# Three score visits instead of four for each two groups, in an attention and gated feed-forward kernel

## The chip, the cores and the metric

The kernel runs on one core of one Trainium2 chip. The metric is the device time of one execution in microseconds (us), as the median of several runs. Times "from the block's start" below count from the first gate matmul of a token block.

## The reference

Attention with a sliding window of 128 and four sink tokens for 4 batches of 8 heads, 768 tokens, head size 64. Its output, turned to 3072 tokens of 512 features, goes through a gated feed-forward layer (512 to 1536 and back).

```python
scores = scale * np.matmul(q, k.transpose(0, 1, 3, 2))
keep = is_sink | ((rel >= 0) & (rel < window))        # rel = query - key, window 128
a = softmax(np.where(keep, scores, -1e9))
x = np.matmul(a, v)                                   # to (3072, 512)
g = x @ w_gate
out = (g * sigmoid(g) * (x @ w_val)) @ w_out          # (3072, 512)
```

## The kernel before, in words

**Groups and blocks.** Attention is done in twelve groups of 256 queries (three to a batch: group g is batch g // 3, part c = g % 3). The feed-forward layer is done in eight token blocks of 256 or 512 tokens. A block of 512 has twelve *gate units* (function `gate`) and four *downs* (function `down`). A gate unit projects one chunk of 128 features with the gate weights into a bank `pg` (four matmuls of 512 columns on TensorE, called PE), takes tanh of it on ScalarE (ACT) into `th`, projects with the value weights into `pv`, and on VectorE (DVE) forms `u` from `th` and `pg`, and `ht` from `u` and `pv`. A down sums twelve matmuls over `ht` into `pd`.

**Attention between units.** The work of later groups is put by hand into numbered slots of a block's units. A slot's steps are issued between the two projections of its unit, so in each engine's queue they stand after `pg` and before `pv`. The steps of a group are:

- *Scores*, `step_S` (matmuls at L288, exps at L295, masks at L300). Eight heads are four pairs. Head size 64 fills half of PE's rows, so the two heads of a pair run in the two row halves. Each head has its own PSUM bank `s`. ACT takes exp of each head into `e`; a DVE multiplication by the mask, one for each pair, is put into the list `later`. Groups with c = 0 have no previous keys and take 384 columns for each head where the others take 512.
- *Sink scores*, `step_K` (L316), for groups with c > 0: one bank `pk` and one exp into `es`.
- *Values*, `step_PV` (L351), in four parts (two query tiles j, two halves hh of the heads). For c > 0 the first part also issues the sinks' matmuls (`step_sinks`, L331, 32 rows), which take four banks `o` at once; for c = 0 each part takes its own. DVE then divides (`rcp` L359, `xn` L365), through `later`.
- *Turning* the result, `step_X`: for these groups a transposing DMA on SP's queue from `xn` to `xT`, also through `later`. `xbar` turns a later group's q and k on the same queue.

`gate` calls `flush` after its own DVE work, which issues what is in `later`: masks, divisions and turns stand behind `u` and `ht` of their unit.

**Banks.** All PSUM tiles (`pg`, `pv`, `pd`, `s`, `pk`, `o`) come from one pool of eight banks. A tile that finds none free waits, on PE, for one that is released by its last reader.

**Order around the change.** Blocks 3, 4 and 5 carry groups 5 and 6, 7 and 8, 9 and 10. The order is written by `pair`, into slots:

```python
((s, s + 2), Ss(ga)), (s, [K(ga)]), ((s + 4, s + 5, s + 6, s + 7), PVs(ga)),
((s + 6, s + 8), Ss(gb)), ((s + 8, s + 9), Xs(ga)), (s + 6, [K(gb)]),
(10, 10, 11, 12) PVs(gb), (12, 13) Xs(gb)            # s = 0 everywhere
```

So scores are at units 0, 2, 6 and 8, two pairs of heads at each; the first group's values at 4, 5, 6 and 7; the second's at 10, 11 and the first down. In block 3 the first two units are of half the tokens and twice the features; their costs are alike.

Of the kernel before, what the change touches and what calls it, by code (L numbers as in the profile page):

```python
# [7 lines left out]
FP32 = mybir.dt.float32  # L8
BF16 = mybir.dt.bfloat16
AF = mybir.ActivationFunctionType  # L10
ALU = mybir.AluOpType
# [3 lines left out]
def kernel(  # L15
# [12 lines left out]
    nc = tc.nc  # L28
    P = 128
    B, H, S, D = q.shape  # L30
# [8 lines left out]
    NP2 = H // 2  # L39
    GC = S // 256  # L40
# [10 lines left out]
    scale = 1.0 / float(D) ** 0.5  # L51

    def pool(name, bufs, psum=False):
        if psum:
            return ctx.enter_context(
                tc.tile_pool(name=name, bufs=bufs, space=bass.MemoryType.PSUM))
        return ctx.enter_context(tc.tile_pool(name=name, bufs=bufs))
# [7 lines left out]
    epool = pool("epool", 2)  # L65
# [12 lines left out]
    def bank(shape, dtype, name):  # L78
        return psum.tile(shape, dtype, tag="b", name=name)
# [65 lines left out]
    mask = const.tile([P, 2, 256], BF16)  # L145
    mask0 = const.tile([P, 2, 256], BF16)
# [56 lines left out]
    kTs, qTs, es_t, e_t, xns, xTs = {}, {}, {}, {}, {}, {}  # L203
    later = []

    def flush():
        for f in later:
            f()
        later.clear()
# [60 lines left out]
            op=ALU.mult)  # L270
        vsbs.append(vsb)

    def step_S(g, p2):
        b, c = divmod(g, GC)
        if p2 == 0:
            e_t[g] = epool.tile([P, H, 512], BF16, tag="e", name="e")
        q0 = c * 256
        parts = [(q0, q0, 256, P), (q0 + P, q0 + P, P, 3 * P)]
        if c > 0:
            parts.insert(0, (q0 - P, q0, P, 0))  # L280
        lo = 0 if c > 0 else P
        pss = [bank([P, 512], FP32, "s") for _ in range(4)]
        for pp in range(2):
            p = 2 * p2 + pp
            for kk, qq, n, col in parts:
                for h in range(2):
                    r = slice(h * D, (h + 1) * D)
                    nc.tensor.matmul(  # L288
                        pss[2 * pp + h][:, col:col + n], kTs[b][r, p, kk:kk + P],
                        qTs[b][r, p, qq:qq + n], start=True, stop=True)  # L290
        m = (mask if c > 0 else mask0).rearrange("q (o a) x -> q o (a x)", o=1)
        for pp in range(2):
            h0 = 4 * p2 + 2 * pp
            for h in range(2):
                nc.scalar.activation(  # L295
                    e_t[g][:, h0 + h, lo:512], pss[2 * pp + h][:, lo:512],
                    AF.Exp, scale=scale)

            def dve(e=e_t[g][:, h0:h0 + 2, lo:512]):
                nc.vector.tensor_tensor(  # L300
                    e, e, m[:, :, lo:512].broadcast_to([P, 2, 512 - lo]), op=ALU.mult)
            later.append(dve)

    def step_K(g):
        b, c = divmod(g, GC)
        if c == 0:
            return
        ps = bank([P, P], FP32, "pk")
        kfl = kss.rearrange("q b p x -> q b (p x)")
        for a in range(2):  # L310
            for j in range(2):
                for hh in range(2):
                    r, p = 32 * (2 * j + hh), 2 * hh + a
                    t0 = c * 256 + j * P
                    k0 = (KW + 2 * NS) * p - 2 * NS * a
                    nc.tensor.matmul(  # L316
                        ps[r:r + KW], kfl[:, b, k0:k0 + KW], qTs[b][:, p, t0:t0 + P],
                        start=(a == 0), stop=(a == 1), skip_group_check=True)
        es_t[g] = espool.tile([P, P], BF16, tag="es", name="es")
        nc.scalar.activation(es_t[g], ps, AF.Exp, scale=scale)  # L320
# [54 lines left out]
    def step_X(g, j, evict="v"):  # L375
        t0 = g * 256 + j * P
        tb = max(i for i in range(len(SIZES)) if OFF[i] <= t0)
        off = t0 - OFF[tb]
        if tb == 0 and off == 0:
            xTs["01"] = xtp.tile([P, DMC, 512], BF16, tag="xT", name="xT")  # L380
            xTs[0], xTs[1] = (xTs["01"][:, :, 256 * i:256 * (i + 1)] for i in range(2))
        elif tb > 1 and off == 0:
            xTs[tb] = dense(xtp.tile([P, DMC * 512], BF16, tag="xT", name="xT"),
                            DMC, SIZES[tb])
            if tb == 3:
                for i in range(2):
                    xTs[tb, i] = xTs[tb][:, :, 256 * i:256 * (i + 1)]
        if g not in PEX:
            def sp():
                nc.sync.dma_start_transpose(xTs[tb][:, :, off:off + P], xns[g, j])  # L390
            later.append(sp)
            return
        pt = bank([P, DMC, P], BF16, "px")
        for i in range(DMC):
            nc.tensor.transpose(pt[:, i], xns[g, j][:, i * P:(i + 1) * P], ident)

        if evict == "a":
            nc.scalar.copy(out=xTs[tb][:, :, off:off + P], in_=pt)
            return

        def dve():
            nc.vector.tensor_copy(out=xTs[tb][:, :, off:off + P], in_=pt)
        if evict == "now":
            dve()
        else:
            later.append(dve)
# [99 lines left out]
    def gates(tb):  # L506
        return [(gate, tb, f) for f in range(0, DFC, 512 // SIZES[tb])]

    def downs(tb):
        return [(down, tb, t) for t in range(SIZES[tb] // P)]  # L510

    def A(fn, *a):
        return lambda: fn(*a)
# [2 lines left out]
        return [A(step_TN, g, i, j, evict) for j in range(2) for i in range(2)]  # L516

    def Ss(g):
        return [A(step_S, g, p2) for p2 in range(2)]

    def PVs(g):
        return [A(step_PV, g, j, hh) for hh in range(2) for j in range(2)]

    def Xs(g):
        return [A(step_X, g, j) for j in range(2)]
# [11 lines left out]
    def K(g):  # L537
        return A(step_K, g)

    def weave(us, slots):  # L540
        assert all(i < len(us) for i in slots)
        for i, (fn, tb, x) in enumerate(us):
            fn(tb, x, slots.get(i, []))

    def slots(*pairs):
        sl = {}
        for at, steps in pairs:
            for i, step in zip(at if isinstance(at, tuple) else (at,) * len(steps),
                               steps):
                sl.setdefault(i, []).append(step)  # L550
        return sl
# [92 lines left out]
    step_PV(0, 0, 0)  # L644
    step_PV(0, 0, 1)
    flush()
    step_S(1, 0)
    masks1 = list(later)
    later.clear()
    step_PV(0, 1, 0)  # L650
# [2 lines left out]
    step_X(0, 0)  # L653
    flush()
    step_X(0, 1, "now")
    step_S(1, 1)
    step_K(1)
    later[:0] = masks1
    flush()
# [12 lines left out]
    def NV(g):  # L672
        return L(A(load_nat, g), A(load_v, g))

    weave(us, slots(
        (4, TN(2)[::2]), (5, TN(2)[1::2]), ((6, 7), Ss(2)), (6, [K(2)]),
        ((8, 8), PVs(2)[:2]), (9, [A(step_PV, 2, 0, 1, "a"), A(step_PV, 2, 1, 1, "a")]),
        ((10, 11), [A(step_X, 2, 0, "a"), A(step_X, 2, 1, "a")]),
        (11, [NV(4), lambda: nc.gpsimd.tensor_copy(out=vcl[64:128], in_=vcl[0:64])]),
        ((14, 14, 15, 15), TN(3, "aa")),  # L680
        (15, [A(xbar, 4)]), (15, [NV(5)]), (19, [A(xbar, 5)]),
        ((17, 18), Ss(3)), (18, [A(step_ks, 1)]), (18, [A(step_vsb, 1)]),
        ((19, 19, 19, 20), PVs(3)), (20, Xs(3)),
        (19, [L(Ss(4)[0], K(4))]), (20, Ss(4)[1:]),
        ((21, 21, 21, 22), PVs(4)), (21, Xs(4)[:1]),
        (22, [Xs(4)[1], flush, A(behind, 3, 383), A(load_nat, 6)]),
        (23, [A(xbar, 6), A(turned, 6), A(load_v, 6), NV(7)])))

    def pair(ga, gb, sh=0):
        s = sh  # L690
        return [((s, s + 2), Ss(ga)), (s, [K(ga)]),
                ((s + 4, s + 5, s + 6, s + 7), PVs(ga)),
                ((s + 6, s + 8), Ss(gb)), ((s + 8, s + 9), Xs(ga)), (s + 6, [K(gb)]),
                ((12, 12, 13, 13) if s else (10, 10, 11, 12), PVs(gb)),
                ((14, 14) if s else (12, 13), Xs(gb))]

    weave([(gate, (3, i), 0) for i in range(2)] + gates(3)[2:] + downs(3), slots(
        (15, [A(step_ks, 2), A(step_vsb, 2)]), *pair(5, 6), (9, [flush, A(xbar, 7)]),
        (13, [flush, A(behind, 4, 511), NV(8)]),
        (15, [A(xbar, 8)]), (15, [NV(9)])))  # L700
    weave(gates(4) + downs(4), slots(
        *pair(7, 8), (3, [A(xbar, 9)]), (15, [A(step_ks, 3), A(step_vsb, 3)]),
        (3, [NV(10)]), (15, [A(xbar, 10)]), (15, [NV(11)])))
    weave(gates(5) + downs(5), slots(*pair(9, 10), (6, [A(xbar, 11)])))
    us = gates(6) + gates(7) + downs(6) + downs(7)
    us[-1] = (lambda tb, t, a: down(tb, t, a, True), *us[-1][1:])
    weave(us, slots(
# [36 lines left out]
```

## Time and profile before

| | us |
|---|---|
| median of 4 runs | 238.38 (237.97 to 238.97) |
| the profiled execution | 239.01 |
| its span, first to last instruction | 237.2 |
| gate units of block 3, from 75.73 to 101.07 | 25.34 |
| gate units of block 4, from 111.67 to 138.11 | 26.44 |
| gate units of block 5, from 148.72 to 173.89 | 25.17 |
| downs after each of them | 10.60 |

The profile gives each engine's instructions in order of time. In a timeline line the columns are the start in us, the time covered, engine and source line, operation, output and input with shapes, the count of instructions merged, and in square brackets the idle time before it with what ended it. PEld is PE's loading of weights. The TensorE clock granted is 1.0 throughout. Matmuls overlap in the pipeline, so a start is surer than an end: costs of PE are read from start to start.

### The profile page before, as it was taken

How to read it: one execution, taken by the hardware profiler on the slowest of the kernel's cores; microseconds unless marked ns; L12 is line 12 of the kernel's file. 1: busy time of each engine (PE TensorE's matmuls, PEld its weight loads, DVE VectorE, ACT ScalarE, POOL GpSimd, SP SyncE). 2: the span in 40 equal slices, each digit the busy share in tenths (PEclk: the TensorE clock that was granted, in tenths of full speed). 3: DMA queues.
4: the chain of work that ended last, by engine and by line, in shares of the span. 5: the costliest groups of instructions: out<-in, count | busy, mean ns of one | idle time of the engine just before them, and what ended most of it. 6: DMA issues, size and time to landing. Idle time of an engine off the chain costs nothing.

```text
span 237.2 us, 4880 instructions
## 1 busy us (share of the span) xinstructions
PE 229.6 (97%) x1867; PEld 128.0 (54%) x1893; DVE 157.6 (66%) x333; ACT 113.6 (48%) x235; POOL 74.9 (32%) x100
## 2 busy tenths in 40 slices
PE   7999999999999999999999999999999999999994
PEld 4677645696555644444444544444444445488443
DVE  3897889677651898970798980688970598877000
ACT  3795475556552845512845622655622663333221
POOL 8985875722602307403526350080000000000000
PEclk9999999999999999999999999999999999999999
DMA  7999999994998968995999997599204100200132
GB/s 136 160 182 177 182 198 205 157 145 73 152 231 150 149 74 56 151 129 162 135 128 129 137 144 154 137 92 143 44 16 137 70 3 0 44 4 0 45 133 91
DMA packets 108743, 27.62 MB, mean 116 GB/s; under 512 B 95792, under 2 KB 105776, under 8 KB 108720
## 3 DMA queue, kind: packets, MB, share of 16 engines
q0 software_dynamic: 76640, 13.90, 76.9%
q1 hardware_dynamic: 30672, 11.58, 25.5%
q10 hardware_dynamic: 1408, 1.84, 2.5%
q8 instruction: 15, 0.25, 0.4%
q14 instruction: 8, 0.07, 0.1%
HBM read 28.34 MB, written 6.29 MB: 146 GB/s over the span
## 4 chain that ended last, share of the span: by engine, by line
PE 91%; DVE 2%; DMA 2%; ACT 1%; issue 1%; SPq 0%; DVEq 0%; ACTq 0%
PE pv L416 26%; PE pd L496 26%; PE pg L416 25%; PE o L351 4%; PE s L288 4%; DMA st<-in_k_dram 2%; DVE xn L365 1%; PE pt L572 1%; PE pt L226 1%; PE o L331 1%; PE pn L241 1%; PE pk L316 1%; ACT th L436 1%; PE s L589 1%; DVE rcp L359 0%
## 5 line engine op out<-in xcount | busy, mean ns | idle before, releaser
L444 DVE SCALAR_TENSOR_TENSOR u<-th,pg 128x512 bf16<-128x512 f32 x72 | 49.2, 684 | 39.2 <-ACT th L436 39.2
L416 PE MATMUL pg<-xT,wg 128*128 128x512 bf16 (+1 forms) x353 | 73.4, 336 | 0.7
L436 ACT ACTIVATE th<-pg 128x512 f32<-128x512 f32 x72 | 43.5, 604 | 63.0 <-PE pg L416 58.2
L416 PE MATMUL pv<-xT,wv 128*128 128x512 bf16 (+1 forms) x349 | 72.8, 335 | 0.6 <-ACT e L295 0.2
L496 PE MATMUL pd<-wo,ht 128*128 128x512 bf16 (+2 forms) x292 | 64.5, 370 | 0.5 <-issue 0.2
L416 PEld LDWEIGHTS <-wg 128*128 128x128 bf16 x360 | 35.1, 98 | 27.7 <-issue 0.4
L455 DVE TENSOR_TENSOR ht<-u,pv 128x512 bf16<-128x512 bf16 x62 | 42.7, 688 | 9.4 <-PE pv L416 2.5
L295 ACT ACTIVATE e<-s 128x512 bf16<-128x512 f32 (+1 forms) x88 | 42.8, 581 | 3.7 <-PE s L288 3.5
L496 PEld LDWEIGHTS <-ht 128*128 128x128 bf16 x300 | 27.8, 97 | 30.3 <-issue 0.3
L416 PEld LDWEIGHTS <-wv 128*128 128x128 bf16 x360 | 32.1, 98 | 20.3 <-issue 1.7
L501 ACT ACTIVATE ot<-pd 128x512 f32<-128x512 f32 (+1 forms) x24 | 14.3, 596 | 46.9 <-PE pd L496 42.9
L111 POOL DMA_DIRECT2D nat<-in_k_dram x20 | 17.7, 891 | 40.2 <-DMA qT<-nat 36.5
L300 DVE TENSOR_TENSOR e<-e,mask 128x1024 bf16<-128x1024 bf16 (+1 forms) x44 | 27.0, 650 | 3.7 <-ACT e L295 3.7
L122 POOL DMA_DIRECT2D va<-in_v_dram x24 | 21.5, 917 | 4.7 <-DMA wo<-in_moe_w_out_dram 2.4
L365 DVE TENSOR_TENSOR xn<-o,rcp 128x256 bf16<-128x256 f32 x44 | 18.7, 425 | 1.5
L351 PEld LDWEIGHTS <-e 128*128 128x128 bf16 x352 | 15.0, 98 | 7.8 <-issue 0.2
L111 POOL DMA_DIRECT2D nat<-in_q_dram x20 | 17.7, 899 | 1.7 <-DMA va<-in_v_dram 0.5
L351 PE MATMUL o<-va,e 128*128 128x65 bf16 x352 | 17.0, 193 | 0.1
L288 PE MATMUL s<-qT,kT 64*128 64x128 bf16 (+1 forms) x240 | 12.9, 237 | 0.0
L288 PEld LDWEIGHTS <-kT 64*128 64x128 bf16 x240 | 7.8, 94 | 7.3 <-issue 6.4
L503 DVE TENSOR_SCALAR ot<-pd 128x128 f32<-128x128 f32 x1 | 0.3, 292 | 14.3 <-PE pd L496 14.3
L359 DVE RECIPROCAL rcp<-o 128x4 f32<-128x4 f32 x48 | 8.3, 175 | 1.4 <-PE o L351 1.3
(74 smaller groups left out, 94.5 us busy)
## 6 DMA issues: line engine op xcount, KB each, us to landing
out_dram<-ot SPq DMA_DIRECT2D x17, 256.0 KB
va<-in_v_dram POOLq DMA_DIRECT2D x24, 128.0 KB, 6.1
nat<-in_k_dram POOLq DMA_DIRECT2D x20, 128.0 KB, 5.0
nat<-in_q_dram POOLq DMA_DIRECT2D x20, 128.0 KB, 5.5
wg<-in_moe_w_gate_dram POOLq DMA_DIRECT2D x6, 256.0 KB, 8.3
wv<-in_moe_w_val_dram POOLq DMA_DIRECT2D x6, 256.0 KB, 8.6
wo<-in_moe_w_out_dram POOLq DMA_DIRECT2D x4, 384.0 KB, 11.1
out_dram<-ot ACTq DMA_DIRECT2D x6, 256.0 KB
```

The costliest lines, as they stand in the source:

```text
L111: nc.gpsimd.dma_start(x[:, i, j].rearrange("p (h d) -> p h d", d=D), src[b, :, t0:t0 + P].rearrange("h p d -> p h d"))
L122: nc.gpsimd.dma_start(va[:, j, :, 0:D], v[b, :, t0:t0 + P].rearrange("h p d -> p h d"))
L288: nc.tensor.matmul(pss[2 * pp + h][:, col:col + n], kTs[b][r, p, kk:kk + P], qTs[b][r, p, qq:qq + n], start=True, stop=True)
L295: nc.scalar.activation(e_t[g][:, h0 + h, lo:512], pss[2 * pp + h][:, lo:512], AF.Exp, scale=scale)
L300: nc.vector.tensor_tensor(e, e, m[:, :, lo:512].broadcast_to([P, 2, 512 - lo]), op=ALU.mult)
L351: nc.tensor.matmul(o, l, r, start=(c == 0 and i == 0), stop=(i == len(mms) - 1), skip_group_check=True)
L365: nc.vector.tensor_tensor(xn, po[:, :, 0:D], rcp.broadcast_to([P, 4, D]), op=ALU.mult)
L416: nc.tensor.matmul(ps[:, i * n:(i + 1) * n], ws[fi][:, c, fo * P:(fo + 1) * P], xTs[tb][:, c], start=(c == 0), stop=(c == DMC - 1))
L436: nc.scalar.activation(th, pg, AF.Tanh, scale=0.5)
L444: nc.vector.scalar_tensor_tensor(u, th, 1.0, pg, op0=ALU.add, op1=ALU.mult)
L455: nc.vector.tensor_tensor(hts[tb][:, f:f + 512 // SIZES[tb]].rearrange("p a n -> p (a n)"), u, pv, op=ALU.mult)
L496: nc.tensor.matmul(po, hts[tb][:, f, ts * P:(ts + 1) * P], wos[f // n][:, f % n, lo:hi], start=(f == 0), stop=(f == DFC - 1))
```

## The change

`step_S` now takes any list of (group, pair of heads). It takes two banks for each pair, all of them ahead of its first matmul, then issues all matmuls, then all exps, and puts one mask for each pair into `later`. Matmuls, exps and masks are the same in number, shape and order within a pair.

For groups 5 to 10 the four visits of two pairs become three visits: pairs 0 to 2 of the first group; its pair 3 with pairs 0 and 1 of the second group; pairs 2 and 3 of the second group. The first visit takes six banks `s`, the second six, the third four.

For blocks 3 and 4 (`late`) the visits stand at units 2, 6 and 9, the first group's values are all at unit 7, the second's at 10 and in the first down, and the sink scores of the second group go with its last visit, at unit 9. For block 5 they stand at units 0, 4 and 8; its first group's values are at 2, 3, 6 and 7. The turning of group 7's q and k moves from unit 9 to 10 of block 3. Groups 1 to 4 and 11 keep two visits of two pairs.

```diff
-    def step_S(g, p2):
-        b, c = divmod(g, GC)
-        if p2 == 0:
-            e_t[g] = epool.tile([P, H, 512], BF16, tag="e", name="e")
...
-        pss = [bank([P, 512], FP32, "s") for _ in range(4)]
+    def step_S(*heads):
+
+        banks = [[bank([P, 512], FP32, "s") for _ in range(2)] for _ in heads]
+        for (g, p), pss in zip(heads, banks):
+            b, c = divmod(g, GC)
+            if g not in e_t:
+                e_t[g] = epool.tile([P, H, 512], BF16, tag="e", name="e")
...
+    def S2(g, p):
+        return A(step_S, (g, p), (g, p + 1))
+
+    def S3(g, n, gb=None, nb=0):
+
+        return A(step_S, *((g, p) for p in range(n, NP2 if nb else n + 3)),
+                 *((gb, p) for p in range(nb)))
...
-    def pair(ga, gb, sh=0):
-        s = sh
-        return [((s, s + 2), Ss(ga)), (s, [K(ga)]),
-                ((s + 4, s + 5, s + 6, s + 7), PVs(ga)),
-                ((s + 6, s + 8), Ss(gb)), ((s + 8, s + 9), Xs(ga)), (s + 6, [K(gb)]),
-                ((12, 12, 13, 13) if s else (10, 10, 11, 12), PVs(gb)),
-                ((14, 14) if s else (12, 13), Xs(gb))]
+    def pair(ga, gb, late):
+
+        if late:
+            return [(2, [S3(ga, 0), K(ga)]), (6, [S3(ga, 3, gb, 2)]), ((7,) * 4, PVs(ga)),
+                    ((9, 9), [S2(gb, 2), K(gb)]), ((9, 10), Xs(ga)),
+                    ((10, 10, 12, 12), PVs(gb)), ((12, 13), Xs(gb))]
+        return [(0, [S3(ga, 0), K(ga)]), (4, [S3(ga, 3, gb, 2)]), ((2, 3, 6, 7), PVs(ga)),
+                ((8, 8), [S2(gb, 2), K(gb)]), ((8, 9), Xs(ga)),
+                ((10, 10, 11, 12), PVs(gb)), ((12, 13), Xs(gb))]
...
-        (15, [A(step_ks, 2), A(step_vsb, 2)]), *pair(5, 6), (9, [flush, A(xbar, 7)]),
+        (15, [A(step_ks, 2), A(step_vsb, 2)]), *pair(5, 6, True), (10, [flush, A(xbar, 7)]),
...
-        *pair(7, 8), (3, [A(xbar, 9)]), (15, [A(step_ks, 3), A(step_vsb, 3)]),
+        *pair(7, 8, True), (3, [A(xbar, 9)]), (15, [A(step_ks, 3), A(step_vsb, 3)]),
...
-    weave(gates(5) + downs(5), slots(*pair(9, 10), (6, [A(xbar, 11)])))
+    weave(gates(5) + downs(5), slots(*pair(9, 10, False), (6, [A(xbar, 11)])))
```

More of the change, by code (lines that the diff above doesn't have):

```diff
@@ L271, in step_vsb @@
         vsbs.append(vsb)
-    def step_S(g, p2):
-        b, c = divmod(g, GC)
-        if p2 == 0:
-            e_t[g] = epool.tile([P, H, 512], BF16, tag="e", name="e")
[L277 to L281, printed above, removed]
-        pss = [bank([P, 512], FP32, "s") for _ in range(4)]
-        for pp in range(2):
-            p = 2 * p2 + pp
+    def step_S(*heads):
[4 more added lines that the diff above has]
+                e_t[g] = epool.tile([P, H, 512], BF16, tag="e", name="e")
+            q0 = c * 256
+            parts = [(q0, q0, 256, P), (q0 + P, q0 + P, P, 3 * P)]
+            if c > 0:
+                parts.insert(0, (q0 - P, q0, P, 0))
             for kk, qq, n, col in parts:
@@ L288, in step_S, with dve @@
                     nc.tensor.matmul(
-                        pss[2 * pp + h][:, col:col + n], kTs[b][r, p, kk:kk + P],
+                        pss[h][:, col:col + n], kTs[b][r, p, kk:kk + P],
                         qTs[b][r, p, qq:qq + n], start=True, stop=True)
-        m = (mask if c > 0 else mask0).rearrange("q (o a) x -> q o (a x)", o=1)
-        for pp in range(2):
-            h0 = 4 * p2 + 2 * pp
+        for (g, p), pss in zip(heads, banks):
+            c = g % GC
+            lo = 0 if c > 0 else P
+            m = (mask if c > 0 else mask0).rearrange("q (o a) x -> q o (a x)", o=1)
             for h in range(2):
                 nc.scalar.activation(
[L296 to L301, printed above, removed]
+                    e_t[g][:, 2 * p + h, lo:512], pss[h][:, lo:512], AF.Exp, scale=scale)
+            def dve(e=e_t[g][:, 2 * p:2 * p + 2, lo:512], m=m[:, :, lo:512]):
+                nc.vector.tensor_tensor(e, e, m.broadcast_to(list(e.shape)), op=ALU.mult)
             later.append(dve)
@@ L518, in Ss @@
     def Ss(g):
-        return [A(step_S, g, p2) for p2 in range(2)]
+        return [S2(g, 0), S2(g, 2)]
+    def S2(g, p):
[3 more added lines that the diff above has]
+                 *((gb, p) for p in range(nb)))
     def PVs(g):
@@ L646 @@
     flush()
-    step_S(1, 0)
+    step_S((1, 0), (1, 1))
     masks1 = list(later)
@@ L655 @@
     step_X(0, 1, "now")
-    step_S(1, 1)
+    step_S((1, 2), (1, 3))
     step_K(1)
```

## The prediction

> **What bounds the kernel now.** I read the page first: engine shares, then the chain that ended last.
>
> ```profile
> PE 229.6 (97%) x1867; PEld 128.0 (54%) x1893; DVE 157.6 (66%) x333; ACT 113.6 (48%) x235; POOL 74.9 (32%) x100
> PE 91%; DVE 2%; DMA 2%; ACT 1%; issue 1%; SPq 0%; DVEq 0%; ACTq 0%
> ```
>
> TensorE (PE) is busy 97% of the span and is 91% of the chain. So only PE's own time and the few places where PE stands still can move the end. DVE's 66% hides an uneven load, so next the windows view over the twelve gate units of token blocks 3, 4 and 5 (columns: length, then PE, PEld, DVE, ACT, POOL busy):
>
> ```profile
> 75.73:101.07 25.34, 25.02 (x209) 13.64 (x212) 20.86 (x39) 14.72 (x30) 10.58 (x13) 1.00 1.31 106
> 111.67:138.11 26.44, 26.05 (x221) 12.78 (x224) 21.89 (x42) 15.69 (x31) 12.97 (x16) 1.00 1.61 129
> 148.72:173.89 25.17, 24.96 (x193) 12.06 (x196) 21.36 (x41) 14.80 (x30) 5.25 (x6) 1.00 0.98 94
> ```
>
> In these stretches DVE is over 80% busy and starts 1.7 us after PE, so it trails PE closely. Then the PE timeline of block 4: a visit of two pairs of heads alone, and the one visit where PE stood.
>
> ```profile
> 116.01 1.03 PE L416 MATMUL pg<-xT,wg 128*128 128x512 bf16 x4
> 116.97 0.62 PE L288 MATMUL s<-qT,kT 64*128 64x128 bf16 x12
> 117.52 1.04 PE L416 MATMUL pv<-xT,wv 128*128 128x512 bf16 x4
> ...
> 126.19 0.29 PE L316 MATMUL pk<-qT,kss 128*32 128x128 bf16 x8
> 126.66 0.81 PE L416 MATMUL pv<-xT,wv 128*128 128x512 bf16 x3 [0.17 <-ACT e L295]
> ```
>
> Projections follow each other every 0.864 us (119.25 to 120.11). Four matmuls from 116.01 end at 116.87; the scores start at 116.97: **0.10 us to enter**. Twelve score matmuls, two row halves at once, stream 0.43 us (half of 12 x 170 columns, 0.213 per pair), which ends at 117.40; pv starts at 117.52: **0.12 us to leave**. So a visit costs 0.22 us beside its work.
>
> The stand at 126.66 tells how banks are handed out. From the ACT and PEld timelines of the same block, and of block 3:
>
> ```profile
> 112.74 0.60 ACT L436 ACTIVATE th<-pg 128x512 f32<-128x512 f32 x1 [0.27 <-PE pg L416]
> 113.23 2.06 ACT L295 ACTIVATE e<-s 128x512 bf16<-128x512 f32 x4
> 115.14 0.33 ACT L320 ACTIVATE es<-pk 128x128 bf16<-128x128 f32 x1
> ...
> 126.19 0.12 PEld L316 LDWEIGHTS <-kss 128*32 128x32 bf16 x8 [0.22 <-DVE xn L365]
> ...
> 90.28 0.55 PEld L416 LDWEIGHTS <-wv 128*128 128x128 bf16 x4 [0.33 <-DVE xn L365]
> ```
>
> At unit 6 of block 4 two o banks are held; pg, four s and pk take the other six, pk the one freed last (by xn), and pv must take the first s bank, free after its exp. At unit 6 of block 3, without pk, pv takes that last-freed bank. Both fit one rule: **the bank freed earliest in program order is taken next**. The stands: 0.24 us in block 4 (126.42 to 126.66), 0.18 in block 3 (90.11 to 90.29), 0.05 in block 5 (162.38 to 162.43): 0.47 together.
>
> **What the skill says.** The Trainium skill, "TensorEngine Tiling (Array Packing)", Key Properties: changing the tiling mode drains TensorE. The trace agrees: 0.10 and 0.12 us around score matmuls (64-row mode), and none around value matmuls in 128-row mode (eight cost 0.24 us, sixteen 0.50). The same page, Gotcha 1: row tiling raises PSUM pressure; the three stands above are that. "TensorE: Matmul & The Clock Gate", Architectural detail, says ACT and DVE are strictly first in, first out; in the trace, tanh, exps and masks run in the order written.
>
> **The change, part by part.** T is the end of a unit's pg. Prices: th starts at T+0.20, the first exp at T+0.69, exps every 0.487 us (384 wide: 0.38), the first ending after 0.57; PE then goes on 0.07 later. On DVE u to ht is 0.79, ht to next 0.61, a mask 0.60 (384 wide 0.465), rcp plus xn 0.55.
>
> *Removed:* four score visits per two groups become three: 3 x 0.22 = **-0.66 us**. Score matmuls, exps, masks and K are as many as before. The three old stands go too, their bank pattern being broken: **-0.47 us**.
>
> *First values in one visit (blocks 3, 4):* value visits of 128 rows pay nothing to enter, so merging saves nothing; the sinks' entry and exit stay once.
>
> *Added waits.* Pool of eight banks throughout.
> 1. First visit (unit 2) of blocks 3 and 4: pg + 6 s + pk = 8, so pv takes the first s bank: T + 0.20 + 0.49 + 0.57 + 0.07 = T+1.33. PE is done at T + 0.10 + 0.64 + 0.12 + 0.23 = T+1.09. **2 x 0.24 = 0.48.** Behind pv the whole PE queue waits.
> 2. Middle visit (unit 6): pg + 6 s = 7, pv takes pv's bank of unit 5, free after ht 5. DVE has three masks (1.8 us) more in one lump at unit 2; stepped from there, ht 5 ends some 0.85 us after T: 0.05 and 0.10, **0.15** together.
> 3. Values at unit 7: next pg takes s0, the four sinks take s1 to s4. The fifth exp of block 4 frees at T + 0.69 + 4 x 0.487 + 0.57 + 0.07 = T+3.28; PE arrives at 0.86 + 0.05 + 2 x 0.864 + 0.10 = T+2.74: **0.54**. Block 3, where group 6 is short: T+2.94 against T+2.70: **0.24**. All 32 value matmuls queue behind.
> 4. Last visit (unit 9): four xn (2.2 us) lie in one lump after ht 7, ahead of u 8. In block 4 pv takes pg 8's bank, free after u 8: 21.60 us from the block's start against 21.31 for PE: **0.28**. Block 3 has no pk there, and its bank is free: 0.
> 5. DVE ends later: in block 3 ht 11 at about 28.3 us from the block's start against 28.1 where the first down needs it: **0.23**. Block 4: 28.8 against 29.6, 0.
> 6. Block 5 (visits at 0, 4, 8): in the middle visit the sixth s bank is pv 3's, free after ht 3, which sits behind three masks and one xn: **0.22**; pv behind it takes the bank of the value visit before, xn at 10.0 us: **0.13**; the last pv, behind ht 7: **0.08**.
>
> Sum of waits 0.48 + 0.15 + 0.78 + 0.28 + 0.23 + 0.43 = 2.35; less 0.66 and 0.47: **+1.2 us**. Stepping each block as a whole, in which stands overlap slightly, gives 1.1. I take +1.1.
>
> *Costed at nothing:* Xs of the first group and the transposes of group 7 move one unit later on SP's queue, which at 92.67 already waits for xn; block 4 needs group 7 ten microseconds after. Group 10's transposes are issued by 152.5 (SP timeline) and first used at about 158.5 now: if that cover went, PE would stand for the difference. V and natural loads keep their slots on POOL. e has two buffers, and the earlier group's values are done before each third e, as before.
>
> Uncertain, from both sides: items 2, 4, 5 and 6 (1.09 us) rest on stepped DVE queues; a few tenths less lag makes them nothing (net about +0.1), as much more doubles them (+2.3). Items 1 and 3 use durations shown and stay unless the bank rule is other than I read.
>
> **Rivals.** *Faster: the waits don't come.* If unit 2 and unit 7 get banks that are drained already, only the gains are left: -0.66 to -1.13, 237.3 to 237.7. For it: exps and DVE have half a unit of slack in many units. Against: pool of eight, and 126.66 shows this very wait with four s. It decides once the new waits sum to less than 0.4 us.
> *Nearly even:* items 1 and 3 come, DVE catches up everywhere: +0.1 to +0.5, 238.5 to 238.9. For it: DVE drains its lumps in units 3 to 5 and 10 to 11.
> *Much slower: DVE becomes the bound.* Block 4's DVE work is 12 x 1.40 + 8 x 0.60 + 8 x 0.55 = 26.0 us in 26.4; starting masks two units later loses 0.33 us twice per late block. If the lag is 1 us longer, the downs of blocks 3 and 4 start 0.5 to 1 us late: +2 to +2.3, 240.5.
>
> **How the numbers follow.** The profiled execution took 239.01 us (span 237.2 and 1.8 around it), 0.63 above the median 238.38; the sum is a difference: span 238.3, profiled execution 240.1, median **239.5**. About 0.3% (0.72 us) is what a measurement of this kernel can tell from no change. Chances: bank waits as summed 0.58, much slower 0.07, nearly even 0.22, faster rival 0.13. Slower 0.65, same 0.22, faster 0.13. The likeliest case alone spans 239.1 to 240.2; with the others the range is 237.7 to 240.6.
>
> **What would show it.** In the profile after, three score visits in each of the blocks 3 to 5; PE's pv at unit 2 waiting for an exp by 0.2 us, the sinks of unit 7 waiting for an exp by 0.5 in block 4 and 0.2 in block 3, pv of unit 9 in block 4 waiting for u. Windows of the gate units plus downs should lengthen by about 0.4, 0.6 and 0.2 us. If sinks start 0.1 us after pg, the bank rule is wrong and so is the sign; if the first down stands over 0.5 us, DVE is the bound.

## The result, and the profile after

| | before | after |
|---|---|---|
| median, us | 238.06 (56 runs) | 238.63 (37 runs) |
| ratio to before | | 1.003 (95%: 1.0018 to 1.0042) |
| profiled execution, us | 239.01 | 239.29 |
| its span, us | 237.2 | 237.5 |

The changed kernel is 0.7 us slower (0.003 x 238; the medians differ by 0.57). The forecast had the sign and the kind of cause, and its sum of +1.1 us was too large. From the page of the kernel after, the engine shares and the chain that ended last:

```profile
PE 228.4 (96%) x1867; PEld 127.3 (54%) x1893; DVE 157.8 (66%) x333; ACT 113.6 (48%) x235; POOL 74.9 (32%) x100
PE 83%; DVE 6%; DMA 3%; POOL 2%; issue 2%; ACT 2%; DVEq 0%; POOLq 0%; ACTq 0%
```

PE does the same 1867 matmuls in 1.2 us less busy time, in a longer span. In the chain 8 points have gone from PE to others. These points are lengths of the chain, not time lost. DMA's and POOL's are at the start of the kernel, where inputs came later in this execution. DVE's 6% are nearly all in two stretches, from 82.19 to 88.86 us in block 3 and from 151.46 to 158.84 in block 5: there the chain goes back along DVE's queue from two stands of PE that took 0.13 and 0.40 us (items 2 and 6 of the forecast).

The start varies: block 3 began between 73.84 and 75.73 us in the profiled executions of this study, with the work before it unchanged. So kernels are compared below by the length of blocks 3, 4 and 5 in one profiled execution of each, from first gate to the next block's first gate. The windows view of after, gates and downs of blocks 3 and 4, then the gates of block 5:

```profile
75.44:100.63 25.19, 24.75 (x206) 13.68 (x209) 20.52 (x41) 14.70 (x30) 10.89 (x14) 1.00 1.27 117
100.63:111.52 10.89, 10.84 (x61) 4.98 (x61) 4.41 (x14) 1.79 (x3) 1.45 (x3) 1.00 0.52 133
111.52:137.98 26.46, 25.69 (x214) 12.59 (x216) 21.85 (x42) 15.72 (x31) 13.34 (x16) 1.00 1.51 131
137.98:148.83 10.85, 10.80 (x65) 5.19 (x65) 3.63 (x13) 1.79 (x3) 1.16 (x2) 1.00 1.14 147
148.83:174.19 25.36, 24.97 (x194) 12.13 (x196) 21.58 (x43) 14.62 (x30) 5.26 (x6) 1.00 0.92 94
```

The first pair of numbers is the window, then come its length and PE's busy time. In block 4 PE is idle 0.77 us of the gates, before 0.39. The downs are 0.29 and 0.24 us longer than before. The value matmuls moved into the first down explain 0.12 and 0.24 of this; 0.17 us in block 3 are a stand.

| kernel | ratio to before (95%) | block 3 | block 4 | block 5 | sum, us |
|---|---|---|---|---|---|
| before | | 35.94 | 37.05 | 35.78 | 108.77 |
| after | 1.003 (1.0018 to 1.0042) | 36.08 | 37.31 | 35.96 | 109.35 |
| e1_k_first | 0.9994 (0.9979 to 1.0009) | 35.87 | 36.76 | 35.94 | 108.57 |
| e2_block5 | 1.0015 (0.9995 to 1.0034) | 35.95 | 37.04 | 35.95 | 108.94 |
| e3_one_values | 1.006 (1.0039 to 1.008) | 36.45 | 37.43 | 35.77 | 109.65 |
| e4_single | 1.0101 (1.008 to 1.0121) | 36.62 | 37.60 | 36.58 | 110.80 |
| e5_k_first_34 | 0.9985 (0.9966 to 1.0004) | 37.74 | 36.77 | 35.78 | 110.29 |
| e6_unit0 | 0.998 (0.9967 to 0.9994) | 35.86 | 36.76 | 35.78 | 108.40 |
| e7_block5_unit5 | 0.9991 (0.9977 to 1.0006) | 36.38 | 36.76 | 35.72 | 108.86 |
| e8_values_and_unit9 | 0.9989 (0.9972 to 1.0005) | 36.06 | 36.75 | 35.78 | 108.59 |
| e9_all | 0.9988 (0.9962 to 1.0013) | 36.20 | 36.76 | 35.72 | 108.68 |
| e10_unit0_k_last | 1.0023 (1.0006 to 1.0039) | 36.17 | 37.31 | 35.96 | 109.44 |

The blocks of after are 0.58 us longer than those of before: 0.14, 0.26 and 0.18. The PE timeline of after, block 4: the end of the visit of unit 2, the middle visit, the sinks of unit 7, the end of the visit of unit 9.

```profile
116.70 0.30 PE L314 MATMUL pk<-qT,kss 128*32 128x128 bf16 x8
117.17 1.02 PE L414 MATMUL pv<-xT,wv 128*128 128x512 bf16 x3 [0.18 <-ACT e L295]
...
124.17 0.84 PE L287 MATMUL s<-qT,kT 64*128 64x128 bf16 x18
124.96 1.02 PE L414 MATMUL pv<-xT,wv 128*128 128x512 bf16 x3
...
126.78 0.37 PE L329 MATMUL o<-vsb,es 32*128 32x260 bf16 x4
127.08 1.15 PE L349 MATMUL o<-va,e 128*128 128x65 bf16 x32
...
132.17 0.29 PE L314 MATMUL pk<-qT,kss 128*32 128x128 bf16 x8
132.85 1.02 PE L414 MATMUL pv<-xT,wv 128*128 128x512 bf16 x4 [0.38 <-ACT e L295]
```

Eight pk matmuls take 0.23 us where nothing stands (114.12 to 114.35 in experiment 1). So PE was ready at 116.93 and went on at 117.17 (0.24 us), and was ready at 132.40 and went on at 132.85 (**0.45 us**), both times right after the first exp of the visit (the lines name ACT, L295). The sinks, though, start at 126.78, and their row covers 0.37 us where an undelayed one covers 0.29: a stand of 0.07 to 0.08, not the 0.54 that was forecast.

### The profile page after: what moved, and what is told of

It is laid out like the page before. It is cut to its first block, busy times and chain, and to the rows that moved or that the text cites. A ratio compares the mean times of both kernels' runs of the same rounds, so it can differ in the third digit from the quotient of the medians.

```text
span 237.5 us, 4882 instructions
## 1 busy us (share of the span) xinstructions
PE 228.4 (96%) x1867; PEld 127.3 (54%) x1893; DVE 157.8 (66%) x333; ACT 113.6 (48%) x235; POOL 74.9 (32%) x100
## 4 chain that ended last, share of the span: by engine, by line
PE 83%; DVE 6%; DMA 3%; POOL 2%; issue 2%; ACT 2%; DVEq 0%; POOLq 0%; ACTq 0%
PE pd L494 26%; PE pv L414 24%; PE pg L414 23%; PE o L349 4%; PE s L287 3%; DMA va<-in_v_dram 3%; DVE ht L453 2%; DVE u L442 2%; DVE e L299 1%; DVE xn L363 1%; POOL rows L100 1%; PE o L329 1%; PE pn L241 1%; POOL x L186 1%; ACT e L295 1%
## 5 line engine op out<-in xcount | busy, mean ns | idle before, releaser
L414 PEld LDWEIGHTS <-wv 128*128 128x128 bf16 x360 | 33.0, 98 | 22.1 <-issue 1.6
L295 ACT ACTIVATE e<-s 128x512 bf16<-128x512 f32 (+1 forms) x88 | 42.5, 585 | 4.3 <-PE s L287 4.2
L349 PEld LDWEIGHTS <-e 128*128 128x128 bf16 x352 | 14.3, 98 | 7.1 <-issue 1.0
L349 PE MATMUL o<-va,e 128*128 128x65 bf16 x352 | 16.2, 194 | 0.6 <-DMA va<-in_v_dram 0.5
```

The costliest lines, as they stand in the source:

```text
L295: nc.scalar.activation(e_t[g][:, 2 * p + h, lo:512], pss[h][:, lo:512], AF.Exp, scale=scale)
L349: nc.tensor.matmul(o, l, r, start=(c == 0 and i == 0), stop=(i == len(mms) - 1), skip_group_check=True)
L414: nc.tensor.matmul(ps[:, i * n:(i + 1) * n], ws[fi][:, c, fo * P:(fo + 1) * P], xTs[tb][:, c], start=(c == 0), stop=(c == DMC - 1))
```

## The experiments

The theory: the change saves PE one entry and exit for each two groups, and pays with stands of PE for banks that are still being read. The main rival: DVE is made late by masks and divisions in lumps, and banks are beside the point.

**1. Sink scores ahead of the scores.**

```diff
-            return [(2, [S3(ga, 0), K(ga)]), (6, [S3(ga, 3, gb, 2)]), ((7,) * 4, PVs(ga)),
-                    ((9, 9), [S2(gb, 2), K(gb)]), ((9, 10), Xs(ga)),
+            return [(2, [K(ga), S3(ga, 0)]), (6, [S3(ga, 3, gb, 2)]), ((7,) * 4, PVs(ga)),
+                    ((9, 9), [K(gb), S2(gb, 2)]), ((9, 10), Xs(ga)),
```

> The changed kernel with one edit: the sink scores stand ahead of the scores in their slot (units 2 and 9 of blocks 3 and 4, 8 of block 5), so the short exp of pk runs first and its bank is the first of the visit to come free. Bank theory (the cost of the change is PE waiting for a bank behind big visits): the trace after shows pv of unit 2 standing 0.25 us in each of blocks 3 and 4 and pv of unit 9 of block 4 standing 0.45; pk's bank is free at T + 0.20 + 0.49 + 0.33 + 0.07 = T+1.09, when PE is done at unit 2 (stand about 0) and 0.21 after it at unit 9. So 0.5 + 0.24 = 0.7 us less than the changed kernel: about -0.1 us against the kernel before, ratio 0.9995 to 1.000. Rival, late DVE (masks and divisions in lumps push u and ht back, whatever the banks): nothing changes, ratio stays 1.003.

Measured: 0.9994, blocks 0.78 us shorter than in the changed kernel. The PE timeline of this run, block 4, unit 2:

```profile
113.16 1.03 PE L414 MATMUL pg<-xT,wg 128*128 128x512 bf16 x4
114.12 0.29 PE L314 MATMUL pk<-qT,kss 128*32 128x128 bf16 x8
114.35 0.84 PE L287 MATMUL s<-qT,kT 64*128 64x128 bf16 x18
115.12 1.04 PE L414 MATMUL pv<-xT,wv 128*128 128x512 bf16 x4
```

T is 113.16 + 0.864 = 114.02, and pv starts at T+1.10: no stand. At unit 9 of block 4 the stand of 0.45 us became 0.15. Only the order of two steps was changed, with the same masks and divisions on DVE, and the loss went. The stands behind the exp are shown to be the larger part of the cost; late DVE, as the cause of that part, is refuted.

**2. Block 5 alone.** The pair of groups 5 and 6 and that of 7 and 8 keep four visits at their old places.

```diff
-        ... *pair(5, 6, True), (10, [flush, A(xbar, 7)]),
+        ... *pair_old(5, 6), (9, [flush, A(xbar, 7)]),
-        *pair(7, 8, True), ...
+        *pair_old(7, 8), ...
```

> Three visits in block 5 alone (units 0, 4, 8, first group's values at 2, 3, 6, 7); blocks 3 and 4 as before. Bank theory: the stands in the middle visit (0.40 us) and the last (0.05) against one visit less (0.22) and the old stand (0.05): +0.18 us, ratio 1.0007, and block 5 with its downs 0.18 us longer than before in the trace. Rival, the late places of units 2, 6 and 9 are the cost: block 5 alone is 0.2 us faster than before, ratio 0.999.

Measured: block 5 is 0.17 us longer, the others are as before to 0.01; 1.0015 holds this (1.0007) and no change. The trace decides it. The same middle visit in the trace of after:

```profile
157.77 0.94 PE L287 MATMUL s<-qT,kT 64*128 64x256 bf16 x16
158.88 1.04 PE L414 MATMUL pv<-xT,wv 128*128 128x512 bf16 x3 [0.18 <-DVE xn L363]
```

The visit's work and exit are 0.59 + 0.12 us, so pv could have started at 158.48; it stood 0.40 us in all for banks that ht 3 and a division give back.

**3. The first group's values in one visit, alone.** The kernel before, in blocks 3 and 4:

```diff
-                ((s + 4, s + 5, s + 6, s + 7), PVs(ga)),
+                ((7,) * 4 if one else (4, 5, 6, 7), PVs(ga)),
```

> The kernel before with one part of the change alone: in blocks 3 and 4 the first group's values all at unit 7 (four visits of scores stay at 0, 2, 6, 8). Bank theory: no o bank is held over the score visit of unit 6, so the old stands of 0.18 (block 3) and 0.24 us (block 4) go; at unit 7 the sinks' banks are free by T+2.3, PE arrives at T+2.7: no new stand. -0.4 us, ratio 0.998. Rival, late DVE: four divisions in one lump (2.2 us) ahead of u 8 hold up banks at unit 8: +0.2 to +0.5 us, ratio 1.001 to 1.002.

Measured: 1.006. My expectation was wrong, the rival's sign right, and the trace shows its place. PE and PEld of unit 8, block 3:

```profile
93.80 0.87 PE L288 MATMUL s<-qT,kT 64*128 64x256 bf16 x8
94.93 1.02 PE L416 MATMUL pv<-xT,wv 128*128 128x512 bf16 x4 [0.26 <-ACT e L295]
...
94.33 0.11 PEld L288 LDWEIGHTS <-kT 64*128 64x128 bf16 x3 [0.32 <-DVE xn L365]
```

The old stand of unit 6 is gone (pv at 88.94, the scores' work and exit done at 88.94). But one unit after the values the next visit needs banks that the four divisions still hold: the scores stand for xn, the exps come late, and pv, which takes an s bank, stands behind them. From T = 93.70 a clean visit gives pv at 94.24; it came at 94.93: 0.69 us, in block 4 0.68. Bank waits again, with DVE as the reader that is late. The blocks show 0.88 us of the 1.4; this execution also stood 0.83 us for `xT` ahead of block 3, outside the blocks' lengths, and the rest of the 1.4 stays open.

**4. One pair of heads to a visit.** The kernel before, twelve visits more.

```diff
-                ((0, 2), Ss(ga)), ... ((6, 8), Ss(gb)),
+                ((0, 1, 2, 3), S1s(ga)), ... ((6, 7, 8, 9), S1s(gb)),
```

> The kernel before with each score visit of groups 5 to 10 cut in two (one pair of heads at each of units 0 to 3 and 6 to 9): 12 visits more, all else in its place. If a visit costs 0.22 us of entering and leaving, +2.6 us, less up to 0.4 for stands that smaller visits avoid: +2.2 to +2.6, ratio 1.009 to 1.011. If entering and leaving is hidden behind other work: within 0.3 us, ratio 1.000 to 1.001.

Measured: 1.0101, +2.4 us, of which the blocks show 2.03. Block 5, with hardly any stands on either side, is 0.80 us longer for four more visits: **0.20 us each**; blocks 3 and 4, whose old stands of 0.18 and 0.24 are gone here and have to be added back, give 0.21 and 0.20. The saving of a visit is real, and 0.22 was near enough.

**5. Sink scores first, blocks 3 and 4 alone.** Block 5 is as before; the lines are against experiment 1.

```diff
-    weave(gates(5) + downs(5), slots(*pair(9, 10, False), (6, [A(xbar, 11)])))
+    weave(gates(5) + downs(5), slots(*pair_old(9, 10), (6, [A(xbar, 11)])))
```

> Three visits with the sink scores first in blocks 3 and 4 (the places of the change), block 5 with four visits as before. In the trace of the run with the sink scores first, blocks 3 and 4 with their downs took 72.63 us where the kernel before took 72.99; block 5 is that of before. Bank theory: -0.36 us, ratio 0.9985. Rival, late DVE: blocks 3 and 4 no better than in the changed kernel, +0.4 us, ratio 1.0015.

Measured: 0.9985 as expected, with an interval that just holds 1. Its profiled execution has a block 3 of 37.74 us. The first half units in its PE timeline:

```profile
76.05 1.04 PE L414 MATMUL pv<-xT,wv 128*128 128x256 bf16 x8
78.81 1.03 PE L414 MATMUL pg<-xT,wg 128*128 128x256 bf16 x8 [1.73 <-DMA xT<-xn]
```

The second half unit needs the last turned `xT`. In the kernel before, a score visit with sink scores (0.88 us) stood in unit 0 and covered it. The change took that cover away, which I had not priced. After's own execution shows no stand there (77.18, right behind pv). Read from start to start, this one shows 1.89 us (the view's 1.73 is PE's idle time alone) and that of e7 0.37. How much it costs in the mean isn't settled by single executions.

**6. First visit back at unit 0.** On top of experiment 5:

```diff
-            return [(2, [K(ga), S3(ga, 0)]), (6,
+            return [(0, [K(ga), S3(ga, 0)]), (6,
```

> As the run before it in this list, but the first visit of blocks 3 and 4 at unit 0, where the kernel before had it, not at unit 2. DVE then masks two units earlier, when the trace shows it idle 0.25 us in each unit. If the stand of block 3's first down for ht (0.48 us of weight loading idle, some 0.17 us beyond the work moved there) and the 0.13 us at the middle visit come from DVE starting late, they go: -0.3 us more, ratio 0.9973. If they come from the lump of divisions at unit 7 alone, the place of the first visit changes nothing: ratio 0.9985.

Measured: 0.998, the only version whose interval lies below 1. Blocks 3 and 4 took 35.86 and 36.76 us, as with unit 2 (35.87 and 36.76 in e1). Inside block 3 two things cancel. The stand of the middle visit is gone: from its scores to pv are 0.66 us, in experiment 5 0.78. But pv of unit 0 came at T+1.21, not at T+1.09, behind the exp of pk: ACT was issuing an output transfer of the block before (75.25 to 75.59 us) and began tanh only 0.40 us after T. So masks two units earlier do take away the middle visit's 0.12 us, and nothing is left of it in sum. The downs of block 3 stay at 10.90 us: their stand comes from what is later in the block.

**7. Block 5 with the middle visit at unit 5.** On top of experiment 1:

```diff
-        return [(0, [K(ga), S3(ga, 0)]), (4, [S3(ga, 3, gb, 2)]), ((2, 3, 6, 7), PVs(ga)),
+        return [(0, [K(ga), S3(ga, 0)]), (5, [S3(ga, 3, gb, 2)]), ((2, 3, 7, 7), PVs(ga)),
```

> Three visits with the sink scores first in all three blocks; in block 5 the middle visit at unit 5 instead of 4 and the first group's last values both at unit 7. The stand of 0.40 us at unit 4 came from the banks of ht 3 and of the value visit of unit 3, which are drained one unit later: block 5 with its downs 35.55 us against 35.94 with the visit at unit 4 and 35.78 before. All in all -0.2 - 0.4 = -0.6 us, ratio 0.9975. Rival: the stand only moves to the next visit (values at unit 7 waiting for masks of unit 5): -0.2 us, ratio 0.999.

Measured: 0.9991. Block 5 is 35.72 us, 0.22 less than with the visit at unit 4 where 0.39 was expected: part of the stand moved to unit 8, where the twelve score matmuls cover 0.77 us and not 0.62. The ratio is nearer to the rival's 0.999 than to the expected 0.9975. Block 3 is 0.51 us longer than in experiment 1: 0.33 of it is a longer stand for `xT`, 0.17 a stand in the middle visit, of which experiment 9 shows the cause.

**8. Values in one visit, and the last score visit one unit later.** On top of experiment 3:

```diff
-                ((s + 6, s + 8), Ss(gb)),
+                ((6, 9 if one else 8), Ss(gb)),
```

> The kernel before with the first group's values of blocks 3 and 4 all at unit 7, as in the run that took 1.006, but the last score visit one unit later, at 9. There the trace showed scores of unit 8 standing behind o banks (0.3 to 0.4 us, four divisions in a lump) and pv after them behind an exp (0.26 and 0.31 us). One unit later the o banks are drained: those stands go and so do the old ones of unit 6 (0.18 and 0.24): -0.4 us, ratio 0.998. Rival: the lump of divisions holds up u and ht for longer than a unit, and the stand moves on: ratio 1.002 or more.

Measured: 0.9989, in place of 1.006. The stands at unit 8 went. Gates of block 3 are 0.16 us and block 4 is 0.30 us shorter than before, as expected; but the downs of block 3 are 0.28 us longer, since `ht` of the last unit comes late. With the visit at 8 (experiment 3) they were not, so this stand belongs to the late last visit. A unit between the values and the next visit is worth 0.66 and 0.67 us of the gates of the two blocks, and 0.39 and 0.68 us of the whole blocks. The rival is right in part: in block 3 some of what DVE is late with is paid at the first down.

**9. The parts that gained, together** (edits 6 and 7).

> Three visits in all three blocks, sink scores first, first visits at unit 0, block 5 with its middle visit at unit 5: the parts that gained, together. From the traces: blocks 3 and 4 took 72.62 us with their downs (before 72.99), block 5 took 35.72 (before 35.78), so -0.43 us, ratio 0.998. If parts disturb each other, or what is gained is given back at the next block, 0.999 to 1.000.

Measured: 0.9988 (0.9962 to 1.0013), not better than edit 6 alone. Blocks 4 and 5 are as added up. Block 3 is 0.34 us longer than in e6, with the same order of work in it. Its middle visit (PE), the last transpose of group 6 (SP), and the POOL instruction that reads its result:

```profile
87.44 0.40 PE L287 MATMUL s<-qT,kT 64*128 64x128 bf16 x6
88.00 0.51 PE L287 MATMUL s<-qT,kT 64*128 64x256 bf16 x8 [0.17 <-DVE ht L453]
...
85.46 1.22 SPq L255 DMA_TRANSPOSE qT<-nat  x1
...
88.04 0.18 POOL L541 CAST warmed<-qT 1x1 f32<-1x1 bf16 x1 [7.16 <-DMA qT<-nat]
```

Group 5's pair ran; group 6's waited until 88.00. The trace names ht, but ht 5 ended at 87.93 in this execution and equally 0.59 us after T in e6, where nothing stood. What differs is the transpose: issued at 85.46 here, at 83.83 in e6. POOL's instruction stands for that transfer and went on at 88.04, within 0.04 us of the scores. In e1 and e7 group 6's scores stood too, by 0.10 and 0.26 us, and in all three runs they start 2.54 us after the last transpose was issued (84.13 to 86.67, 85.42 to 87.96, 85.46 to 88.00); in e7 ht 5 ended only after that, at 88.19. In after, e5, e6 and e10 they start 2.90 us or more after it, and nothing stands ahead of them. So this is a second transfer whose cover became thin.

**10. The changed kernel, first visit at unit 0, sink scores still last.**

```diff
-            return [(2, [S3(ga, 0), K(ga)]), (6,
+            return [(0, [S3(ga, 0), K(ga)]), (6,
```

> The changed kernel with one edit: the first visit of blocks 3 and 4 at unit 0, the sink scores still after the scores. Bank theory: pv of unit 0 stands 0.24 us behind the first exp as it did at unit 2, pv of unit 9 in block 4 stands 0.45, and nothing else changes: the three blocks take 109.35 us as in the changed kernel (before 108.77), ratio 1.0025. What unit 0 can win is only that the second half unit of block 3 no longer starts 0.88 us earlier, where other runs of this order stood 0.20 to 1.73 us for the turned xT: at most 0.1 us in the mean. Rival, the late places are the cost: ratio 1.000 or less.

Measured: 1.0023 and 109.44 us, as expected. Together with experiments 1, 5 and 6 this separates the two edits: the order within a visit is worth some 0.7 us, the unit it stands in little.

## Why the prediction was right or wrong

| step | forecast, us | in the trace of after, us |
|---|---|---|
| three visits fewer | -0.66 | -0.6 to -0.66 (0.20 to 0.22 each, e4) |
| old stands gone | -0.47 | -0.47 |
| 1. pv of unit 2, two blocks | 0.48 | 0.25 + 0.24 |
| 2. pv of unit 6, blocks 3 and 4 | 0.10 + 0.05 | 0.13 + 0.03 |
| 3. sinks of unit 7, blocks 4 and 3 | 0.54 + 0.24 | **0.07 + 0** |
| 4. pv of unit 9, block 4 | 0.28 | **0.45** |
| 5. first down of block 3 | 0.23 | 0.17 |
| 6. block 5 | 0.43 | 0.40 + 0.05 |
| sum | +1.2 | about +0.66 (blocks: +0.58) |

**Right:** the sign, the drain's price, and items 1, 2, 5 and 6. Item 5 is seen on PEld: of the 10.89 us of the first downs, 0.12 is moved work and 0.17 a stand; weights run ahead, so their own idle time is longer.

```profile
103.52 7.67 PEld L494 LDWEIGHTS <-ht 128*128 128x128 bf16 x37 [0.48 <-DVE ht L453]
```

**Wrong: the bank rule behind item 3**, "the bank freed earliest in program order is taken next", taken in the order in which the kernel is written. Two stands of the kernel before fitted it, but other orders fit them as well, and I did not ask which. The banks are fixed in the program as built. There pg of unit 7 in block 4 lies in the bank of s0, and the four sinks in those of pg 6, s1, s2 and s3. The built program's own list of instructions interleaves the engines. Of the 340 tiles after the first eight, all but 12 take the bank whose last reader stands first in that list, and u 6 stands there between the first and the second exp of unit 6. The readers' times in the trace of after come in the same order. On ACT:

```profile
124.27 0.60 ACT L434 ACTIVATE th<-pg 128x512 f32<-128x512 f32 x1 [1.13 <-PE pg L414]
124.77 3.04 ACT L295 ACTIVATE e<-s 128x512 bf16<-128x512 f32 x6
```

The first exp ends at 124.77 + 0.57 = 125.34 and the second at 125.83; u 6 on DVE ran from 124.90 to 125.59, between them. So pg 6's bank comes second, though its reader is written later than the exps, and the sinks need the fourth exp (124.77 + 3 x 0.487 + 0.57 + 0.07 = 126.87), not the fifth. PE comes to them at 126.78. The shift by one bank is 0.49 us of the forecast's excess in block 4, and 0.24 in block 3. This rests on the trace and the program's banks; no run was made for it alone. The prediction had said what would show this: if sinks start 0.1 us after pg, "the bank rule is wrong and so is the sign". They do start so (126.68 to 126.78), and the rule was wrong. But the kernel still became slower, not faster: without item 3 the forecast's own sum is +0.4.

Item 4 had the right place and the wrong reader for the same reason: pv of unit 9 takes not pg 8's bank but the first s bank, and stands to T+1.33 as in item 1: 131.51 + 1.33 = 132.84, measured 132.85.

So two errors of the bank rule partly cancel: item 4 was 0.17 us too small, item 3 some 0.7 us too large.

**Not in the prediction:** the transfers that were covered in block 3 (experiments 5, 7 and 9). I had asked which transposes the moved visits need, but not which transfer the moved visit had hidden.

**The rivals.** "The waits don't come" is out: items 1 and 4 are there. "DVE becomes the bound" is out as the main cause (experiment 1), but DVE has its part: of the new waits in the table about 1.0 us stand behind exps and 0.8 behind DVE (items 2, 5 and 6), and experiments 3 and 8 show that a lump of divisions does set banks free late. "Nearly even" (+0.1 to +0.5) had its size about right, for another reason than the one it gave: not DVE catching up, but one bank's shift at the sinks.

## What to carry to other kernels

When steps that each take a bank are merged into a larger visit, count the banks up to the next matmul of the main stream and ask which reader frees the bank that it takes; look the bank up in the built program, since the written order gave the wrong one here. Put the step with the shortest reader first in the visit, which here turned +0.7 us into about none without removing any work. Leave a unit between a lump of work on the reading engine and the next visit that needs its banks. And when a step is moved, look for the transfer that its time was covering, at the old place as well as at the new one.

## What the runs showed of the hardware

Going from 128-row matmuls to 64-row ones and back costs PE 0.20 to 0.22 us beside the work, in every block, and sixteen value matmuls in 128-row mode cost twice eight (0.48 to 0.49 us against 0.24). The turned q of group 6 could be used by PE 2.54 us after its last transposing transfer was issued, the same in three executions. The start of block 3 moved by up to 1.9 us between profiled executions that do the same work ahead of it, more than the change itself; lengths of blocks agree to 0.01 us where nothing stood, and so told apart what spans could not.
